# A sliding-window attention and token mixer in one kernel: the value products ordered by half with the next scores behind them, and no 64-row matrix work in token mixing

## The chip, the cores and the metric

The kernel runs on one core of a Trainium2 chip. Its time is the device time of one execution in microseconds. Five engines matter: TensorE (PE in the profile; its weight loads are listed as PEld), VectorE (DVE), ScalarE (ACT), GpSimd (POOL), and SyncE (SP), which issues most DMAs. Each engine works through its own list of instructions in the order in which the program writes them, and waits for the others by semaphores. Matrix products go to PSUM, which has eight banks here shared out to tiles by tag; a tile with one buffer must be read out before the next one of that tag is written.

## The reference

`B, H, S, D = 8, 8, 576, 64`. Attention looks back 64 positions, and its result, laid out as `x` with 8 x 576 rows of 512 channels, goes through a token mixer and a channel mixer:

```python
scores = q @ k.transpose(0, 1, 3, 2) / sqrt(D)
mask = (rel >= 0) & (rel < 64)                  # rel = row - column
attn = softmax(where(mask, scores, -1e9))
x = (attn @ v).transpose(0, 2, 1, 3).reshape(B, S, H * D)
h = relu(x.transpose(0, 2, 1) @ w_tok1) @ w_tok2        # d_tok = 256
u = x + h.transpose(0, 2, 1)
out = u + relu(u @ w_ch1) @ w_ch2                       # d_ch = 1536
```

The weights come as 64-bit floats and are converted to 32-bit ones in the kernel.

## The kernel before

The first stage (some 295 us) does attention and token mixing; the second (L574 to L621) the channel mixer, in nine chunks of 512 rows, L582 and L618 on TensorE.

The first stage goes over 36 tiles. A tile has 128 rows: two blocks of 64 positions, of one batch or, for every ninth tile (`i % 9 == 4`), the last block of each of two batches. So a pair of batches has nine tiles, and the fifth belongs half to either.

The order is written out by hand in the loop at L451 to L523, and nothing reorders it. Turn `i` of that loop mixes the work of neighbouring tiles. Before the change TensorE's list in one turn is:

- the scores of tile `i+1` (`qk`, L257, written to the two tiles `s`; 64-row, 64-column products);
- the transposition of the first half of tile `i`'s exponentials (`pt_transpose`, L292, into `pp`; ScalarE copies it to `pt`, L294); a half is four heads, even or odd ones;
- a piece of the second token product (`tok2`): transpositions of `x` (L383) and six products (L390) into the one-buffer tile `up`, which ScalarE copies to `u` (L395);
- the transposition of the second half;
- the first token product of tile `i-1` (`tok1`, L348), which needs `x` of that tile split in a high part (ScalarE, L91) and a low part (POOL, L94);
- the value products of tile `i` (`av`, L304, into `xp`), 16 of them, each on 64 columns of the array;
- a second piece.

There are 64 pieces, eight per batch. A piece of the first half covers 256 positions: two full transpositions. One of the second half covers 320: two full ones and one of 64 rows of the shared fifth tile. Where a batch ends or begins, the shared tile also enters `tok1`: one of its `tok1` products, with the low part of the weights, works on 64 rows only.

Between these, VectorE does mask and maxima (L274, L277), sums, the division by them (L318) and, in two turns of three, steps of the weight conversion (L179 to L194); ScalarE does exponentials (L285), copies and casts; POOL does low parts and a conversion step (L196). All matrix work uses 32-bit operands, with high and low parts for the token and channel products.

What the steps of the prediction touch: `av` and its heads (L302), `tok1_part` (L336 to L349), `tok2` (L378 to L384), and the place of `qk` in the loop (L466).

Of the kernel before, what the change touches and what calls it, by code (L numbers as in the profile page):

```python
# [74 lines left out]
def mixer_kernel(ctx: ExitStack, tc: tile.TileContext, qh, kh, vh, wt1, wt2, wc1, wc2, out):  # L75
# [37 lines left out]
    with ExitStack() as actx:  # L113
# [26 lines left out]
        maskr = [pa.tile([P, P], F32R, name=f"maskr{m}") for m in range(2)]  # L140
        identr = pa.tile([P, P], F32R, name="identr")
        make_identity(nc, ident)
        nc.scalar.copy(identr, ident)
        for m in (1, 0):
# [9 lines left out]
            nc.scalar.activation(maskr[m], mask[m], AF.Copy, scale=NEG_PE / NEG)  # L154

        t1hi = pa.tile([P, 5 * DT], F32R, name="t1hi")
        t1lo = pa.tile([P, 5 * DT], F32R, name="t1lo")
# [70 lines left out]
        def job_finish():  # L228
            if to_finish:
                n, w = to_finish.pop(0)  # L230
                finished.add(n)
                src, hi, lo, o, m = jobs[n]
                if hi is None:
                    nc.sync.dma_start(w2_dram[:, o:o + m], w)
                else:
                    eng = nc.vector if src is wt2 or n >= N_FIRST else nc.gpsimd
                    split(nc.scalar, eng, hi[:, o:o + m], lo[:, o:o + m], w)

        s_ps, e_sb, st = {}, {}, {}
# [59 lines left out]
        def av(i, pts):  # L299
            vt = loaded.pop(i)[1]  # L300
            xp = ps.tile([P, H, D], F32, name=f"xp{i}", tag="av", bufs=1)
            for h in range(H):  # L302
                for half in range(2):
                    nc.tensor.matmul(xp[half * BLK:(half + 1) * BLK, h],  # L304
                                     pts[h % 2][:, h // 2, half * BLK:(half + 1) * BLK],
                                     vt[:, half, h], start=True, stop=True)
            return xp
# [29 lines left out]
        def tok1_part(i, b, rows, slot, first, last):  # L337
# [3 lines left out]
            for tt in range(NTT):  # L341
                if rows is full:
                    combos = ((t1hi, xhi, full), (t1hi, xlo, full), (t1lo, xhi, full))
                else:
                    x = xhi if rows is top else xlo
                    combos = ((t1hi, x, full), (t1lo, x, rows))
                for n, (w, x, r) in enumerate(combos):
                    nc.tensor.matmul(h_ps[b][tt], w[r, slot * DT + tt * P:slot * DT + (tt + 1) * P], x[r],  # L348
                                     start=first and n == 0, stop=last and n == len(combos) - 1)  # L349
# [20 lines left out]
        def tok2(b, half, ct, hh):  # L370
# [6 lines left out]
            cs = slice(ct * P, (ct + 1) * P)  # L377
            segs = [(base + 2 * half + j, slice(0, P), j * P, P) for j in range(2)]  # L378
            if half == 1:
                r = slice(BLK, P) if odd else slice(0, BLK)  # L380
                segs.append((p * TPP + 4, r, 256, BLK))
            for j, (i, rows, o, m) in enumerate(segs):
                nc.tensor.matmul(up[:, o:o + m], xs[i][rows, cs], ident[rows, rows],  # L383
                                 start=(j == 0), stop=False, is_transpose=True, skip_group_check=True)  # L384
# [62 lines left out]
        for i in range(TOK1_FROM, NT + 1):  # L447
            m = min(n + (1 if i < TOK1_SLOW else 2), i)
            tok1_plan[i] = range(n, m)
            n = m  # L450
        for i in range(-1, NT + 1):  # L451
            if 0 <= i and i + 2 < NT:
# [12 lines left out]
            early = i < N_EARLY  # L465
            if i + 1 < NT:  # L466
                qk(i + 1)
            if 0 <= i < NT:
# [35 lines left out]
            if 0 <= i < NT:  # L504
# [3 lines left out]
                else:  # L508
                    norm(i, xp, ri)
            run_pieces(min(have, n_pieces[1]))  # L510
            for n in tok1_plan.get(i + 1, ()):
# [148 lines left out]
```

## Time and profile before

| what | value |
|---|---|
| median of 3 runs | 886.76 us (886.35 to 886.89) |
| profiled execution | 888.41 us |
| its span, first to last instruction | 886.5 us |
| mean granted TensorE clock | 0.994 |
| TensorE busy | 864.6 us, 98% of the span |
| VectorE, ScalarE, POOL busy | 372.3, 311.8, 101.4 us |

A row of the page's groups and of the answers drawn from it names the source line, engine, operation, tiles written and read, and shape; then busy time and mean length, then idle time ahead of it and who ended that. A row of the timeline gives the start in microseconds from the beginning of the span, the length, engine, line, operation, tiles, shape and count; idle time ahead of it stands in brackets with what released it. Matrix products overlap in the pipeline, so the distance from one start to the next says what a product costs, not its length. Row lengths of the chain of waits are what that step added to the chain.

### The profile page before, as it was taken

To read this page: it belongs to the slowest core of one execution; us is meant where nothing else is said; L and a number is where in the kernel's file an instruction comes from. 1 tells how busy PE (TensorE), PEld (TensorE's weight loads), DVE (VectorE), ACT (ScalarE), POOL (GpSimd) and SP (SyncE) were. 2 spreads that over 40 slices of the span, in tenths; PEclk is the share of its full clock that TensorE was granted. 3 is DMA by queue.
4 is the path that set the end of the run, shared out by engine and by line. 5 is a ranking of instruction groups with operands and counts; after the bars stand their busy time and mean duration, and the time that the engine had idled before them with its cause. 6 is when DMAs were issued, how large, how long until landed. Compare 5 with 4: busy or idle time off the path is not lost.

```text
span 886.5 us, 14562 instructions
## 1 busy us (share of the span) xinstructions
PE 864.6 (98%) x6002; PEld 708.6 (80%) x6002; DVE 372.3 (42%) x701; ACT 311.8 (35%) x966; POOL 101.4 (11%) x104
## 2 busy tenths in 40 slices
PE   7899999999999999999999999999999999999998
PEld 4667878778768888888888888888888888888887
DVE  4978777787776598130220220230220220220211
ACT  4878778778776452120120120120120220220200
POOL 2433343333332000000000000000000000000000
PEclk9989999999999999999999999999999999999999
DMA  9557566566554442100100100100100100100001
GB/s 324 188 180 248 180 229 229 196 204 225 199 175 132 130 156 90 59 1 36 60 0 36 60 1 36 60 1 36 60 12 24 60 13 24 60 13 36 0 13 36
DMA packets 39906, 84.69 MB, mean 96 GB/s; under 512 B 5280, under 2 KB 18336, under 8 KB 37920
## 3 DMA queue, kind: packets, MB, share of 16 engines
q1 hardware_dynamic: 37728, 81.93, 27.5%
q10 hardware_dynamic: 2112, 1.84, 0.6%
q8 instruction: 47, 0.77, 0.4%
q14 instruction: 19, 0.16, 0.1%
HBM read 64.09 MB, written 19.66 MB: 94 GB/s over the span
## 4 chain that ended last, share of the span: by engine, by line
PE 84%; DVE 9%; ACT 4%; issue 1%; DMA 1%; SPq 0%; POOL 0%; DVEq 0%; ACTq 0%
PE op L618 33%; PE gp L582 31%; PE up L390 5%; PE xp L304 4%; PE s L257 4%; PE h L348 3%; PE up L383 2%; ACT e L285 2%; PE pp L292 2%; DVE nm L277 1%; DVE e L274 1%; ACT pt L294 1%; DMA k<-kh 1%; DVE r L194 1%; DVE c L191 1%
## 5 line engine op out<-in xcount | busy, mean ns | idle before, releaser
L586 ACT ACTIVATE ghi<-gp 128x512 fp32r<-128x512 f32 x108 | 64.6, 598 | 440.3 <-PE gp L582 439.9
L618 PE MATMUL op<-ghi,w2lo 128*128 128x512 f32 (+1 forms) x444 | 170.3, 384 | 0.2 <-DVE w2lo L94 0.2
L618 PE MATMUL op<-ghi,w2hi 128*128 128x512 f32 (+1 forms) x444 | 170.2, 383 | 0.0
L618 PE MATMUL op<-glo,w2hi 128*128 128x512 f32 (+1 forms) x444 | 170.2, 383 | 0.0
L582 PE MATMUL gp<-uhi,w1hi 128*128 128x512 f32 x432 | 168.1, 389 | 0.0
L582 PE MATMUL gp<-ulo,w1hi 128*128 128x512 f32 x432 | 168.1, 389 | 0.0
L582 PE MATMUL gp<-uhi,w1lo 128*128 128x512 f32 x432 | 168.1, 389 | 0.0
L587 DVE SCALAR_TENSOR_TENSOR glo<-gp,ghi 128x512 fp32r<-128x512 f32 x108 | 74.6, 691 | 190.6 <-ACT ghi L586 190.6
L620 DVE TENSOR_TENSOR uf<-op,uf 128x512 f32<-128x512 f32 (+1 forms) x37 | 25.0, 677 | 242.1 <-PE op L618 242.1
L618 PEld LDWEIGHTS op<-ghi,w2lo 128*128 128x128 f32 x444 | 83.5, 188 | 17.0 <-DVE w2lo L94 0.6
L618 PEld LDWEIGHTS op<-glo,w2hi 128*128 128x128 f32 x444 | 83.5, 188 | 16.4
L618 PEld LDWEIGHTS op<-ghi,w2hi 128*128 128x128 f32 x444 | 83.5, 188 | 16.3
L285 ACT ACTIVATE e<-e,nm 128x128 f32<-128x128 f32 x232 | 90.4, 393 | 13.9 <-DVE nm L277 11.4
L582 PEld LDWEIGHTS gp<-uhi,w1lo 128*128 128x128 f32 x432 | 81.1, 188 | 16.9
L582 PEld LDWEIGHTS gp<-ulo,w1hi 128*128 128x128 f32 x432 | 81.1, 188 | 16.8
L582 PEld LDWEIGHTS gp<-uhi,w1hi 128*128 128x128 f32 x432 | 81.1, 188 | 16.8
L304 PEld LDWEIGHTS xp<-v,pt 128*64 128x64 f32 x1152 | 41.0, 143 | 21.6 <-ACT pt L294 9.5
L304 PE MATMUL xp<-v,pt 128*64 128x64 f32 x1152 | 48.7, 234 | 6.4 <-ACT pt L294 6.0
L274 DVE SCALAR_TENSOR_TENSOR e<-s,mask 128x512 f32<-128x512 f32 x58 | 39.5, 680 | 26.7 <-PE s L257 26.7
L294 ACT COPY pt<-pp 128x512 f32<-128x512 f32 x72 | 41.7, 584 | 22.1 <-PE pp L292 21.7
L94 POOL TENSOR_TENSOR xlo<-x,xhi 128x512 fp32r<-128x512 f32 x32 | 41.2, 1287 | 55.5 <-ACT xhi L91 55.3
L257 PE MATMUL s<-k,q 64*64 64x128 f32 x1152 | 45.8, 295 | 1.4 <-DMA k<-kh 0.7
(72 smaller groups left out, 1000.0 us busy)
## 6 DMA issues: line engine op xcount, KB each, us to landing
v<-vh SPq DMA_DIRECT2D x36, 512.0 KB, 3.7
raw<-wc SPq DMA_DIRECT2D x32, 384.0 KB, 4.4
q<-qh SPq DMA_DIRECT2D x36, 256.0 KB, 4.1
k<-kh SPq DMA_DIRECT2D x7, 1280.0 KB, 7.8
out<-uf SPq DMA_DIRECT2D x35, 256.0 KB, 2.3
uf<-u_dram SPq DMA_DIRECT2D x8, 1024.0 KB, 5.8
u_dram<-u SPq DMA_DIRECT2D x7, 512.0 KB, 4.5
k<-kh SPq DMA_DIRECT2D x5, 256.0 KB, 7.0
```

What stands on the lines that cost most here:

```text
L94: eng_lo.tensor_sub(lo, src, hi.bitcast(F32))
L257: nc.tensor.matmul(s[u][half * BLK:(half + 1) * BLK, j], qt[r, j, half], kbs[b][r, j, n * BLK:n * BLK + P], start=not on_pe, stop=True, sk ...
L274: nc.vector.scalar_tensor_tensor(out=e, in0=s_ps.pop((i, u)), scalar=scale, in1=mk.unsqueeze(1).to_broadcast([P, 4, P]), op0=ALU.mult, op1 ...
L285: nc.scalar.activation(e[:, h], src[:, h], AF.Exp, bias=nm[:, g:g + 1], scale=by, accum_out=sm[:, g:g + 1])
L294: nc.scalar.copy(pt, pp)
L304: nc.tensor.matmul(xp[half * BLK:(half + 1) * BLK, h], pts[h % 2][:, h // 2, half * BLK:(half + 1) * BLK], vt[:, half, h], start=True, sto ...
L348: nc.tensor.matmul(h_ps[b][tt], w[r, slot * DT + tt * P:slot * DT + (tt + 1) * P], x[r], start=first and n == 0, stop=last and n == len(co ...
L390: nc.tensor.matmul(up[:, :n], hx[:, cs], w[:, tt * S + s0:tt * S + s0 + n], start=False, stop=(k == 6), skip_group_check=True)
L582: nc.tensor.matmul(gp, w[:, ct * F + ft * P:ct * F + (ft + 1) * P], x[:, ct], start=(k == 0), stop=(k == 3 * NCT - 1))
L586: nc.scalar.activation(ghi, gp, AF.Relu)
L587: nc.vector.scalar_tensor_tensor(out=glo, in0=gp, scalar=0.0, in1=ghi.bitcast(F32), op0=ALU.max, op1=ALU.subtract)
L618: nc.tensor.matmul(op, w[:, ct, ft], x[:, cols], start=(k == 0), stop=(k == 3 * NFT - 1))
```

## The change

Two things are changed at once.

The value products of a tile are issued with all even heads first, then all odd ones. Even heads need the first transposed half, odd heads the second. And the scores of tile `i+2` are issued at the end of turn `i`, between its value products and its second piece, where the scores of tile `i+1` stood at the start of turn `i+1`, behind that piece. (The scores of tile 0 go ahead of the loop.)

TensorE around the value products of tile 10, before (`xp` value products, `up` a piece, `s12` scores of tile 12, `pp11` a transposition of exponentials; the third and fourth value rows go on in turn):

```order
L304 MATMUL xp10_1338<-v10_1016,pt10_0_1281 64x64 x2
L304 MATMUL xp10_1338<-v10_1016,pt10_1_1315 64x64 x2
...
L383 MATMUL up0_1_3_1357<-ident_65,x2_528 128x128
L383 MATMUL up0_1_3_1357<-ident_65,x3_583 128x128
L383 MATMUL up0_1_3_1357<-ident_65,x4_689 128x64
L390 MATMUL up0_1_3_1357<-t2hi_129,hhi0_0_764 128x320
...
L257 MATMUL s12_0_1380<-k2_703,q12_1136 64x128 x2
L257 MATMUL s12_1_1381<-k2_703,q12_1136 64x128 x2
...
L292 MATMUL pp11_0_1398<-ident_65,e11_0_1285 128x128 x4
L383 MATMUL up1_0_0_1419<-ident_65,x5_799 128x128
```

The same place after:

```order
L313 MATMUL xp10_1345<-v10_1041,pt10_0_1288 64x64 x8
L313 MATMUL xp10_1345<-v10_1041,pt10_1_1322 64x64 x8
L266 MATMUL s12_0_1364<-k2_730,q12_1161 64x128 x2
L266 MATMUL s12_1_1365<-k2_730,q12_1161 64x128 x2
...
L393 MATMUL up0_1_3_1382<-ident_65,x2_533 128x128
L393 MATMUL up0_1_3_1382<-ident_65,x3_590 128x128
L393 MATMUL up0_1_3_1382<-ident_65,x4_696 128x128
L400 MATMUL up0_1_3_1382<-t2hi_134,hhi0_0_771 128x320
...
L301 MATMUL pp11_0_1405<-ident_65,e11_0_1292 128x128 x4
L393 MATMUL up1_0_0_1426<-ident_65,x5_806 128x128
```

The scores stand ahead of the piece now; between it and the next piece (`up1_0_0`) only `pp11_0` is left, and the third transposition has 128 columns.

Token mixing has no 64-row work any more. The third transposition of a second-half piece takes all 128 rows of the shared tile, against the identity or, for the odd batch, a matrix with its halves exchanged (`swapped`); the 64 columns that belong to the other batch are written and not used. In `tok1`, the low part of the weights for the shared tile stands in `t1z`, zero in the other 64 rows, so that this product takes all 128 rows too. TensorE at the shared tile 13, before:

```order
L348 MATMUL h2_0_1320<-xhi13_1715,t1hi_127 128x512
L348 MATMUL h2_0_1320<-xhi13_1715,t1lo_128 128x512
L348 MATMUL h2_1_1321<-xhi13_1715,t1hi_127 128x512
L348 MATMUL h2_1_1321<-xhi13_1715,t1lo_128 128x512
L348 MATMUL h3_0_1917<-xlo13_1716,t1hi_127 128x512
L348 MATMUL h3_0_1917<-xlo13_1716,t1lo_128 128x512
```

and the rows for the second of the two batches after:

```order
L358 MATMUL h3_0_1924<-xlo13_1741,t1hi_132 128x512
L358 MATMUL h3_0_1924<-xlo13_1741,t1z_130 128x512
L358 MATMUL h3_1_1925<-xlo13_1741,t1hi_132 128x512
L358 MATMUL h3_1_1925<-xlo13_1741,t1z_130 128x512
L358 MATMUL h3_0_1924<-xhi14_1870,t1hi_132 128x512
```

Count and place of the products are the same; those of `t1lo` read 64 rows before, those of `t1z` read 128. POOL makes the new constants: two copies and a memset in the setup, and two casts behind the last low part of the token weights:

```order
L94 TENSOR_TENSOR t1lo_133<-w2_364,t1hi_132 128x320
L94 TENSOR_TENSOR xlo1_439<-x1_431,xhi1_438 128x512
L202 TENSOR_TENSOR w3_466<-r3_465,c3_449 128x320
L94 TENSOR_TENSOR t1lo_133<-w3_466,t1hi_132 128x320
L246 CAST t1z_130<-t1lo_133 64x256 x2
L94 TENSOR_TENSOR xlo2_543<-x2_533,xhi2_542 128x512
```

They stand ahead of the low part of tile 2. The lists of ScalarE and VectorE keep their order.

```diff
+        swapped = pa.tile([P, P], F32, name="swapped")
...
+        for c in range(2):
+            nc.gpsimd.tensor_copy(swapped[:, c * BLK:(c + 1) * BLK], ident[:, (1 - c) * BLK:(2 - c) * BLK])
+
+        t1z = pa.tile([P, 2, DT], F32R, name="t1z")
+        nc.gpsimd.memset(t1z.bitcast(F32), 0.0)
...
+                    if src is wt1 and o + m == 5 * DT:
+                        for c, r in enumerate((top, bottom)):
+                            nc.gpsimd.tensor_copy(t1z[r, c], t1lo[r, 4 * DT:].bitcast(F32))
...
-            for h in range(H):
+            for h in [*range(0, H, 2), *range(1, H, 2)]:
...
-                    combos = ((t1hi, xhi, full), (t1hi, xlo, full), (t1lo, xhi, full))
+                    combos = ((t1hi, xhi), (t1hi, xlo), (t1lo, xhi))
                 else:
                     x = xhi if rows is top else xlo
-                    combos = ((t1hi, x, full), (t1lo, x, rows))
-                for n, (w, x, r) in enumerate(combos):
-                    nc.tensor.matmul(h_ps[b][tt], w[r, slot * DT + tt * P:slot * DT + (tt + 1) * P], x[r],
+                    combos = ((t1hi, x), (None, x))
+                for n, (w, x) in enumerate(combos):
+                    w, o = (t1z[:, rows is bottom], 0) if w is None else (w, slot * DT)
+                    nc.tensor.matmul(h_ps[b][tt], w[:, o + tt * P:o + (tt + 1) * P], x,
...
-            segs = [(base + 2 * half + j, slice(0, P), j * P, P) for j in range(2)]
+            segs = [(base + 2 * half + j, ident, j * P) for j in range(2)]
             if half == 1:
-                r = slice(BLK, P) if odd else slice(0, BLK)
-                segs.append((p * TPP + 4, r, 256, BLK))
-            for j, (i, rows, o, m) in enumerate(segs):
-                nc.tensor.matmul(up[:, o:o + m], xs[i][rows, cs], ident[rows, rows],
+
+                segs.append((p * TPP + 4, swapped if odd else ident, 256))
+            for j, (i, perm, o) in enumerate(segs):
+                nc.tensor.matmul(up[:, o:o + P], xs[i][:, cs], perm,
...
+        qk(0)
         for i in range(-1, NT + 1):
...
-            if i + 1 < NT:
-                qk(i + 1)
...
+            if i + 2 < NT:
+                qk(i + 2)
             run_pieces(min(have, n_pieces[1]))
```

## The prediction

> **What bounds the kernel now.** The page came first: busy shares, then the chain that ended last.
>
> ```profile
> PE 864.6 (98%) x6002; PEld 708.6 (80%) x6002; DVE 372.3 (42%) x701; ACT 311.8 (35%) x966; POOL 101.4 (11%) x104
> PE 84%; DVE 9%; ACT 4%; issue 1%; DMA 1%; SPq 0%; POOL 0%; DVEq 0%; ACTq 0%
> ```
>
> TensorE is busy for 98% of the span, but the lines that the change touches (scores L257, value products L304, token products L348, transpositions L383) run only in the first third. So the second view is the busy time by stretch: two single periods (from one tile's scores to the next tile's), then two long stretches.
>
> ```profile
> 69.57:76.73 7.16, 6.76 (x95) 5.71 (x94) 6.05 (x13) 5.38 (x21) 3.23 (x3) 1.00 0.52 167
> 84.52:92.27 7.75, 7.75 (x97) 6.31 (x96) 5.88 (x13) 5.63 (x21) 2.23 (x2) 1.00 0.53 183
> 62.43:183.04 120.61, 117.92 (x1527) 96.55 (x1523) 92.97 (x185) 94.88 (x352) 43.25 (x38) 1.00 0.63 210
> 183.04:294.60 111.56, 107.66 (x1266) 87.42 (x1266) 79.53 (x153) 81.27 (x284) 35.84 (x32) 0.98 0.58 194
> ```
>
> Columns are length, then PE, PEld, DVE, ACT, POOL busy, granted clock, DMA. From 62 to 295 us TensorE is nearly always busy, VectorE and ScalarE for three quarters. There are two kinds of period: light (7.16 us, two pieces of the first half) and heavy (7.75 us, two pieces of the second half, which hold the 64-row transposition). Being busy is not the same as advancing, so the third view is the timeline, where start-to-start distances count. The heavy period:
>
> ```profile
> 84.28 0.31 PE L390 MATMUL up<-t2hi,hlo 128*128 128x320 f32 x1
> 84.52 1.10 PE L257 MATMUL s<-k,q 64*64 64x128 f32 x32
> 85.56 0.66 PE L292 MATMUL pp<-ident,e 128*128 128x128 f32 x4
> 86.05 0.59 PE L383 MATMUL up<-ident,x 128*128 128x128 f32 x3
> 86.82 0.31 PE L390 MATMUL up<-t2lo,hhi 128*128 128x320 f32 x1
> 86.36 0.14 PEld L383 LDWEIGHTS up<-ident,x 64*128 64x128 f32 x1 [0.17 <-issue]
> 89.46 1.24 PE L304 MATMUL xp<-v,pt 128*64 128x64 f32 x32
> 90.63 0.64 PE L383 MATMUL up<-ident,x 128*128 128x128 f32 x3
> 92.03 0.31 PE L390 MATMUL up<-t2hi,hlo 128*128 128x320 f32 x1
> ```
>
> The light period:
>
> ```profile
> 71.10 0.38 PE L383 MATMUL up<-ident,x 128*128 128x128 f32 x2
> 71.44 0.28 PE L390 MATMUL up<-t2lo,hhi 128*128 128x256 f32 x1
> 72.03 0.60 PE L292 MATMUL pp<-ident,e 128*128 128x128 f32 x4
> 72.39 0.48 PE L348 MATMUL h<-xhi,t1hi 128*128 128x512 f32 x1
> 72.70 0.39 PE L348 MATMUL h<-xlo,t1hi 128*128 128x512 f32 x1
> 72.93 0.40 PE L348 MATMUL h<-xhi,t1lo 128*128 128x512 f32 x1
> 73.96 0.34 PE L304 MATMUL xp<-v,pt 128*64 128x64 f32 x4
> 74.69 1.03 PE L304 MATMUL xp<-v,pt 128*64 128x64 f32 x28 [0.40 <-ACT pt L294]
> 75.66 0.44 PE L383 MATMUL up<-ident,x 128*128 128x128 f32 x2
> 76.52 0.28 PE L390 MATMUL up<-t2hi,hlo 128*128 128x256 f32 x1
> ```
>
> **The transposition without 64 rows.** With three transpositions, the last on 64 rows, the first transposition and the second product lie 0.77 us apart (86.05 to 86.82). With two full ones it is 0.34 (71.10 to 71.44). A third full one adds about 0.11 (four L292 rows end to end, less the last one's length: (0.60-0.27)/3) and the wider first product 0.02: 0.47. So each of the 32 pieces concerned gains 0.30 us: 24 in twelve heavy periods, 8 after the last scores. The 64-row weight load waits 0.17 us for nothing the trace names; the rest stands between it and the next product.
>
> The Trainium skill, TensorE: Matmul & The Clock Gate, section "Why this matters for your kernels", speaks against this: products of few rows that land in different row groups run at the same time, so narrow work would be the cheap kind. Here nothing ran beside the 64-row rows (0.77 against 0.34). By the page this term would be a small loss, not 0.30 a piece.
>
> **The token products of half tiles.** Four rows alternate 128 and 64 rows, here after a wait for POOL:
>
> ```profile
> 254.14 0.50 PE L348 MATMUL h<-xhi,t1hi 128*128 128x512 f32 x1 [0.39 <-POOL xhi L330]
> 254.57 0.50 PE L348 MATMUL h<-xhi,t1lo 64*128 64x512 f32 x1
> ```
>
> They follow each other at 0.43 us, full rows at 0.23 (72.70 to 72.93). A group of four gains 0.80, eight groups (two per pair of batches) 6.4. But the wait ahead shows that POOL, ScalarE or the next value products set the end in some of them. Bounds 1.6 to 6.4; I take half, 3.2.
>
> **The next scores behind the value products.** The change takes the scores from behind the second piece to ahead of it. Undisturbed value products with scores right behind:
>
> ```profile
> 61.35 1.15 PE L304 MATMUL xp<-v,pt 128*64 128x64 f32 x32
> 62.43 1.10 PE L257 MATMUL s<-k,q 64*64 64x128 f32 x32
> ```
>
> That is 1.08 us, with no more gap than value products then transpositions have. One change of shape goes away: product to scores takes 0.24 (84.28 to 84.52) against a product's pace of 0.145, and the four L292 rows behind scores 0.66 against 0.60. Gain 0.15 a period. Nothing is issued but matrix rows; no DMA is moved, nor any row of POOL's, SP's, ScalarE's or VectorE's queues. The inputs of the scores are loaded more than a period ahead.
>
> The cost is a new wait. The bank of the pieces ("up") exists once. Today scores and L292 stand between the second piece and the next first one; now L292 alone. ScalarE's rows, the copy in this heavy period and the one before it with a weight cast:
>
> ```profile
> 84.63 0.43 ACT L395 COPY u<-up 128x320 f32<-128x320 f32 x1 [0.26 <-PE up L390]
> 84.95 0.62 ACT L91 CAST xhi<-x 128x512 fp32r<-128x512 f32 x1
> 78.52 0.59 ACT L294 COPY pt<-pp 128x512 f32<-128x512 f32 x1 [0.26 <-PE pp L292]
> 79.00 0.52 ACT L91 CAST w1hi<-w 128x384 fp32r<-128x384 f32 x1
> 79.41 0.40 ACT L285 ACTIVATE e<-e,nm 128x128 f32<-128x128 f32 x1
> 80.97 0.41 ACT L395 COPY u<-up 128x320 f32<-128x320 f32 x1
> 81.28 0.58 ACT L294 COPY pt<-pp 128x512 f32<-128x512 f32 x1
> 78.33 1.28 POOL L94 TENSOR_TENSOR xlo<-x,xhi 128x512 fp32r<-128x512 f32 x1 [0.25 <-ACT xhi L91]
> ```
>
> The copy ends 0.78 us after the last product starts (84.28 to 85.06); L292 is through after 0.15+0.43. So the next first piece waits 0.22 (0.17 with the narrower copy), and L292's second half, token and value products queue behind it.
>
> **Value products by half.** Today they stop after four rows for the second copy: 1.70 us from 73.96 to the transposition at 75.66, against 1.08 undisturbed: 0.62 a light period; in the heavy one 1.17 (89.46 to 90.63), a loss of 0.09. Now the first half (0.47) runs during that copy. Whether the stall goes depends on the copy. Scores earlier by a piece let VectorE (6.05 us busy of 7.16) start its maxima earlier. Then ScalarE's own line-up decides: second piece's copy, cast of x, copy of pt, weight cast, exponentials, first piece's copy, second copy of pt. From the second piece's last product that is 0.35 (84.28 to 84.63) + 0.32 (to 84.95) + 0.52 (0.62 less the overlap seen between neighbours) + 0.48 + 0.41 + 1.56 + 0.31 + 0.58 + 0.05 = 4.58; then the second half of the value products 0.47, change of shape 0.15, scores 1.04 (84.52 to 85.56), and the second piece 1.10 (90.63 to 92.03 less 0.30). This ring is 7.34 us. For a light period it is 4.45+0.47+0.15+1.04+0.86 = 6.97.
>
> Without the weight cast (about two periods in five) other things end last. Heavy: TensorE's own work, 7.75-0.60-0.15-0.09+0.22 = 7.13. Light: the low half of x. It is ready 0.33+0.27+0.62+0.08+1.28 = 2.58 after the last product, and TensorE wants it after 0.12+0.44+0.17+0.93+0.36+0.31 = 2.33, so it stalls 0.25: 7.16-0.62-0.15+0.17+0.25 = 6.81. Today x is ready earlier because the copy ahead of its cast is; that is the stall that comes next.
>
> Sum over the periods: heavy 8x0.41 + 4x0.62 = 5.8; light 5x0.19 + 5x0.35 = 2.7 (two longer light ones are in the token term).
>
> **Setup.** Two copies and a memset on POOL stand ahead of its first addition, for which it waits long anyway; without that cover, three rows no longer than the one below (0.87) would add up to 2.6 us. Two casts into t1z (64x256) stand ahead of a low half of x on POOL, in the stretch where VectorE sets the end:
>
> ```profile
> L94 POOL TENSOR_TENSOR t1lo<-w,t1hi 128x320 fp32r<-128x320 f32 x4 | 3.5, 867 | 8.2 <-ACT t1hi L91 8.2
> 36.19 1.16 DVE nm L272
> 28.24 0.35 DVE nm L272
> ```
>
> By t1lo each cast is at most 0.69 (867 ns x 256/320). The small VectorE row L272 took 1.16 beside POOL's work there, 0.35 elsewhere. So the casts cost between -0.8 (the small row slips in between) and 1.4; I take 0.4.
>
> **The sum.** 5.8 + 2.7 + 3.2 + 2.4 (8x0.30, pieces after the last scores, where the chain is TensorE alone) - 0.4 = 13.7 us. The profiled execution took 888.41, its span 886.5, so it would come to 874.7; the median of the runs shown is 886.76, and the same off it gives **873.1**. The channel stage behind (L582, L618) starts earlier and keeps its length.
>
> **Rivals.** *TensorE's sum comes true entire*: no ring, no waits. 12x0.84 + 10x0.77 + 6.4 + 2.4 + 0.8 = 27: 860. Against it: a 7.34 ring needs only rows that exist. 12%.
>
> *The rings are longer than reckoned*, light periods gain nothing, heavy ones 0.2, token groups a quarter: 2.4+1.6+2.4-1.2 = 5: 881.5. For it: VectorE is busy 6.05 of 7.16 us and may deliver late. 18%.
>
> *Slower: the low half of x.* Its POOL row now falls on VectorE's weight conversion. If the two hold each other up as L272 shows (0.8 us), and the token products wait 1.2 us for it in each of some 16 periods with a conversion, 19 us go: 892. From 1.0 us a period it decides. Against it: VectorE also starts earlier. 6%.
>
> *Narrow work costs nothing of itself*, the page's rule as a mechanism here: the 0.30 stays when the rows are full, so the 64-row terms vanish, wider rows add 32x0.05, and of the order only the light 2.7 is left, heavy periods going even: about 886, no change. The page is the TensorE page of the Trainium skill named above. The 0.77 against 0.34 speaks against it. 3%.
>
> **Chances and range.** My forecast has 61%, from 868 to 878 by itself. The half clock granted for some microseconds where TensorE had waited (0.98 in the last long stretch) may come at other places, 1 or 2 us either way. The range takes the larger part of the two neighbours: 864 to 881.5. A run tells 0.2%, or 1.8 us, from no change: faster 0.89, same 0.04, slower 0.07.
>
> **What would show it.** First transposition to second product 0.47 in heavy pieces; half-tile token rows at 0.23; value products with no stop after four rows; a wait of about 0.2 at L393 for the copy of u; periods near 7.1 to 7.35 and 6.8 to 7.0. Wrong if light periods stay at 7.16 with a new stall at the low half of x, or if the copy of u comes late behind exponentials.

## The result, and the profile after

The changed kernel takes 879.46 us (median; 878.17 to 881.3) where the kernel before took 886.83 us in runs beside it. The ratio is 0.9918, with a 95% interval of 0.9903 to 0.9933: 7.4 us faster. The forecast was 873.1 us, 13.7 us faster, so the sign was right, the time lies in the range (864 to 881.5) near its upper end, and nearly half of the expected gain is missing. The profiled execution took 880.53 us, its span 878.7.

The page's busy shares and the chain that ended last, of the changed kernel:

```profile
PE 850.6 (97%) x6002; PEld 702.6 (80%) x6002; DVE 378.3 (43%) x701; ACT 307.5 (35%) x966; POOL 105.3 (12%) x109
PE 83%; DVE 8%; ACT 4%; POOL 2%; issue 2%; DMA 1%; POOLq 0%; SPq 0%; DVEq 0%; ACTq 0%
```

TensorE has 14.0 us less work (864.6 before), about what was predicted as the gain, but the span fell by 7.8 only: the rest went into waiting. POOL has entered the chain with 2%.

Busy time by stretch, before, then after. The first row of each runs from the end of the value products of tile 24 to that of tile 31 (seven periods whose token products take no shared tile); the second from the first product of chunk 0 of the channel stage to that of chunk 1. The third row of after lies inside its second. Columns as in the prediction.

```profile
197.88:249.84 51.96, 50.82 (x673) 42.08 (x669) 38.82 (x80) 40.70 (x152) 17.22 (x15) 1.00 0.59 204
294.46:360.23 65.77, 65.59 (x290) 53.99 (x289) 50.26 (x106) 22.48 (x44) 0.00 (x0) 1.00 0.32 104
```

```profile
191.21:241.71 50.50, 49.73 (x672) 41.19 (x669) 42.96 (x81) 40.37 (x158) 18.35 (x16) 1.00 0.64 210
283.36:352.44 69.08, 67.22 (x291) 55.15 (x289) 50.05 (x106) 21.94 (x44) 0.00 (x0) 0.98 0.38 116
324.00:328.00 4.00, 4.00 (x11) 3.17 (x12) 3.83 (x10) 0.58 (x2) 0.00 (x0) 0.57 0.24 84
```

The first stage ends 11.10 us earlier (283.36 against 294.46), but the first chunk behind it takes 3.31 us longer. The other chunks keep their length to 0.01 us.

Where a period's time goes is seen in the timeline. This is a light period (both its pieces are of the first half) of the changed kernel, from the last product of its second piece on (tile 25):

```profile
193.27 0.28 PE L400 MATMUL up<-t2hi,hlo 128*128 128x256 f32 x1
193.59 0.37 ACT L405 COPY u<-up 128x256 f32<-128x256 f32 x1 [1.34 <-PE up L400]
193.86 0.62 ACT L91 CAST xhi<-x 128x512 fp32r<-128x512 f32 x1
194.56 1.43 POOL L94 TENSOR_TENSOR xlo<-x,xhi 128x512 fp32r<-128x512 f32 x1 [4.72 <-ACT xhi L91]
195.36 0.47 PE L358 MATMUL h<-xhi,t1hi 128*128 128x512 f32 x1
196.05 0.50 PE L358 MATMUL h<-xlo,t1hi 128*128 128x512 f32 x1 [0.21 <-POOL xlo L94]
197.41 1.15 PE L313 MATMUL xp<-v,pt 128*64 128x64 f32 x32
198.49 1.10 PE L266 MATMUL s<-k,q 64*64 64x128 f32 x32
```

The value products run through, 1.08 us from start to the next scores: their stall is gone. Instead the product of the low half starts 0.69 us behind the one ahead of it, where 0.23 is the pace: a stall of 0.46. Read upwards: the low half waits for its difference on POOL, that for the cast of x on ScalarE, and the cast stands behind the copy of u, for which ScalarE had idled 1.34 us. The product on TensorE that the copy wants comes a scores block later than it used to. The waits for POOL's xlo, by the weight loads, have grown from 2 to 19 (before, then after; columns: us in total, times, longest):

```profile
PEld h L348 <- POOL xlo L94: 2.2, 2, 1.2
```

```profile
PEld h L358 <- POOL xlo L94: 9.6, 19, 1.2
```

For a budget, the table gives the start of each group of TensorE rows to the start of the next group, summed over those seven periods (tiles 24 to 31); a wait ahead of a group counts with the group before it. The granted clock was full in all of these stretches. All kernels of the study that bear on it are in it; e1 to e10 are explained below.

```
us in seven periods      pieces  scores  score transp.  token   value   sum
before                    18.02    7.25      5.94       10.97    9.79   51.96
after                     15.80    7.25      7.02       12.76    7.68   50.50
e2  64-row work only      16.01    7.24      5.93       10.98   10.94   51.10
e5  by half only          18.02    7.25      5.93       10.95    8.32   50.47
e6  scores moved only     17.83    7.24      7.01       12.36    8.25   52.70
e1  both orders           17.83    7.25      7.01       12.26    7.57   51.92
e7  both orders + split   17.83    7.25      7.01       11.00    7.60   50.69
e3  after + split         15.84    7.25      7.33       10.99    7.60   49.00
e9  after - scores moved  15.99    7.24      5.93       11.04    8.48   48.68
e10 e9 + split            16.23    7.25      6.97       10.97    8.28   49.71
```

After against before: pieces -2.2, value products -2.1, but score transpositions +1.1 (the piece behind them waits for the copy of u) and token products +1.8 (the late low half).

The start of the channel stage, changed kernel, by the timeline:

```profile
284.02 0.52 ACTq L420 DMA_DIRECT2D u_dram<-u  x1
286.37 0.60 ACT L597 ACTIVATE ghi<-gp 128x512 fp32r<-128x512 f32 x1 [2.38 <-PE gp L593]
291.24 0.55 ACT L175 ACTIVATE c<-raw 128x384 f32<-128x384 f32 x1 [4.28 <-DMA u_dram<-u]
291.69 0.58 ACT L597 ACTIVATE ghi<-gp 128x512 fp32r<-128x512 f32 x1
323.94 0.50 PE L629 MATMUL op<-ghi,w2lo 128*128 128x512 f32 x1 [1.86 <-DVE w2lo L94]
```

In the kernel before, the same rows stood without that wait:

```profile
295.12 0.52 ACTq L410 DMA_DIRECT2D u_dram<-u  x1
297.40 0.60 ACT L586 ACTIVATE ghi<-gp 128x512 fp32r<-128x512 f32 x1 [2.31 <-PE gp L582]
297.89 0.54 ACT L169 ACTIVATE c<-raw 128x384 f32<-128x384 f32 x1
```

ScalarE's row c does not read u. Its output shares memory with the tile of u that is being stored. The two new tiles (2.5 KB per partition) shift the first stage's tiles, and the compiled program has one more wait there, for the queue of that store: DMAHW6 alone before, now

```
L175 ACTIVATE c27_4425<-raw27_4402 128x384 [waits DMAHW6_49,DMAHW5_49]
```

ScalarE stands at it for 4.28 us, VectorE's weight conversion waits 4.1 us for it, and 33 us later TensorE waits 1.86 us for w2lo. Half clock follows (0.57 in the stretch from 324 to 328 above). The Trainium skill, TensorE: Matmul & The Clock Gate, "What's actually happening", lets the clock fall after an idle window of about 3.4 us; here one wait of 1.86 us stood ahead of it, and in e2_rows below 2.1 us at the same place brought none.

### The profile page after: what moved, and what is told of

It is laid out like the page before. It is cut to its first block, busy times and chain, and to the rows that moved or that the text cites. A ratio compares the mean times of both kernels' runs of the same rounds, so it can differ in the third digit from the quotient of the medians.

```text
span 878.7 us, 14566 instructions
## 1 busy us (share of the span) xinstructions
PE 850.6 (97%) x6002; PEld 702.6 (80%) x6002; DVE 378.3 (43%) x701; ACT 307.5 (35%) x966; POOL 105.3 (12%) x109
## 4 chain that ended last, share of the span: by engine, by line
PE 83%; DVE 8%; ACT 4%; POOL 2%; issue 2%; DMA 1%; POOLq 0%; SPq 0%; DVEq 0%; ACTq 0%
PE op L629 33%; PE gp L593 30%; PE h L358 5%; PE up L400 4%; PE s L266 4%; PE xp L313 3%; PE up L393 2%; POOL xlo L94 2%; PE pp L301 1%; ACT u L405 1%; DVE r L200 1%; DMA u_dram<-u 1%; DVE c L197 1%; ACT xhi L91 1%; ACT e L294 1%
## 5 line engine op out<-in xcount | busy, mean ns | idle before, releaser
L313 PEld LDWEIGHTS xp<-v,pt 128*64 128x64 f32 x1152 | 37.4, 137 | 16.4 <-ACT pt L303 6.3
L266 PE MATMUL s<-k,q 64*64 64x128 f32 x1152 | 43.7, 287 | 2.4 <-DVE c L197 1.9
L313 PE MATMUL xp<-v,pt 128*64 128x64 f32 x1152 | 43.1, 226 | 2.7 <-ACT pt L303 2.4
L294 ACT ACTIVATION_READ_ACCUMULATOR e<-e,nm 128x1 f32 x232 | 44.8, 193 | 0.0
```

The source lines that it names most:

```text
L266: nc.tensor.matmul(s[u][half * BLK:(half + 1) * BLK, j], qt[r, j, half], kbs[b][r, j, n * BLK:n * BLK + P], start=not on_pe, stop=True, sk ...
L294: nc.scalar.activation(e[:, h], src[:, h], AF.Exp, bias=nm[:, g:g + 1], scale=by, accum_out=sm[:, g:g + 1])
L313: nc.tensor.matmul(xp[half * BLK:(half + 1) * BLK, h], pts[h % 2][:, h // 2, half * BLK:(half + 1) * BLK], vt[:, half, h], start=True, sto ...
```

## The experiments

Theory: the orders work on TensorE as predicted, but the cast of x stands behind the second piece's copy on ScalarE, and moving the scores ahead of that piece makes both late; beside that, the new tiles' place costs the first chunk 3.3 us. First rival: VectorE and POOL hold each other up, so x is late wherever its cast stands. Second rival: the channel stage's start is bound by VectorE's weight conversion and loses whatever an earlier start gains.

**The two orders alone (e1_order).**

```
-            for h in range(H):
+            for h in [*range(0, H, 2), *range(1, H, 2)]:
...
+        qk(0)
         for i in range(-1, NT + 1):
...
-            if i + 1 < NT:
-                qk(i + 1)
...
+            if i + 2 < NT:
+                qk(i + 2)
             run_pieces(min(have, n_pieces[1]))
```

> The kernel before with the two changes of order alone: the value products by half and the scores block behind them. The 64-row work stays, and so does the layout of the memory. My theory is that both orders take the wait of the value products away (0.62 us in a light period), that the low half of x is late afterwards because its cast stands behind the copy of the second piece on ScalarE (0.2 to 0.5 us of stall on the token products of a period), and that the first chunk of the channel stage, whose 3.3 us loss in the changed kernel comes from the two new tiles' place in memory, is not touched here: 882 to 884.5 us, with the wait of c27 on ScalarE below 0.5 us and the token products that stall on xlo as in the changed kernel. The first rival (VectorE and POOL hold each other up, whatever the order) gives the same stall in the changed kernel and in the kernel before, so no gain: 886 to 887. The second rival (the channel stage's start loses what any earlier start gains, since VectorE's conversion of the weights bounds it) gives a first chunk longer by whatever the first stage is shorter: 886 to 887 too, but with the end of the first stage 3 us earlier.

Measured: 888.16 us, ratio 1.0016 (1.0006 to 1.0027): the orders alone gain nothing; the time is 3.7 us above the upper end of the expectation. The budget shows why: the value products take 2.2 us less, and the token products and the wait for the copy of u take 2.4 more. Outside the seven periods, those of tiles 32 and 33 take 2.2 us more than before, behind a wait of 1.57 us for POOL's half tile and with half clock from 252.6 to 259.5 us. The first rival has the same stall with either order; here it is the order that moves it. The second rival has no support either: the first chunk keeps its 65.77 us. ScalarE's copies and casts in the seven periods, before and e1_order (the number behind the bar: busy us, mean ns; then the idle time just ahead):

```profile
L395 ACT COPY u<-up 128x256 f32<-128x256 f32 (+1 forms) x14 | 5.4, 388 | 2.9 <-PE up L390 2.9
L91 ACT CAST xhi<-x 128x512 fp32r<-128x512 f32 x7 | 4.4, 622 | 0.2 <-DVE x L318 0.2
```

```profile
L395 ACT COPY u<-up 128x256 f32<-128x256 f32 (+1 forms) x14 | 5.5, 392 | 11.6 <-PE up L390 11.6
L91 ACT CAST xhi<-x 128x512 fp32r<-128x512 f32 x7 | 4.4, 622 | 0.0
```

Nearly all of ScalarE's idle time (11.6 of 12.2 us) now stands ahead of the copy of u. The Trainium skill, TensorE: Matmul & The Clock Gate, "Architectural detail: the array is 16× 32×32, not 1× 128×128", calls ScalarE's queue strict first in, first out; these rows agree: the cast waits for nothing of its own (0.0) while the copy ahead of it waits 11.6 us.

**The 64-row work alone (e2_rows)** is the changed kernel with the two orders undone, as in the diff above read backwards.

> The kernel before with the 64-row work alone replaced; both orders as before. By my theory the PE work shrinks by 0.30 us in each of 32 pieces of token mixing (9.6 us), of which the 8 pieces behind the last tile show in full (2.4 us) and those under a period that PE bounds show in part, and the half-tile token products give up to 3.2 us; the first chunk of the channel stage loses about 3 us through the place of the two new tiles, with the wait of c27 on ScalarE above 3 us: 881.5 to 884.5 us in all. If the loss at the channel stage came from the orders and not from the tiles, the wait would be missing here and the time 879 to 881.5.

Measured: 883.68 us, ratio 0.9961 (0.9946 to 0.9976), inside the expectation. The pieces give 2.0 us in the seven periods, but the value products' stall takes 1.15 of it back: they reach ScalarE's second copy of pt earlier and wait longer. That is why this part and the value products by half are worth more together than apart. The first chunk took 1.94 us longer, with

```profile
ACT c L175 <- DMA u_dram<-u: 4.5, 1, 4.5
PE op L628 <- DVE w2lo L94: 2.1, 1, 2.1
```

The granted clock stayed at 1.00 through this chunk, though TensorE waited longer here than in the changed kernel.

**The casts of x ahead of the second piece (e3_split)**, in the changed kernel:

```
+            for n in tok1_plan.get(i + 1, ()):
+                if n not in xhl:
+                    split_x(n)
             run_pieces(min(have, n_pieces[1]))
-            for n in tok1_plan.get(i + 1, ()):
-                if n not in xhl:
-                    split_x(n)
```

> The changed kernel with the casts and differences of x (split_x) written ahead of the second piece of token mixing, so that the cast stands ahead of that piece's copy on ScalarE. My theory (the low half is late because of the cast's place) says that the stall of the token products on xlo goes below 0.1 us in the periods without a shared tile, and that the time falls by 2 to 5 us from 879.5 to 874.5 to 877.5; the piece's copy then comes up to 0.9 us later and may hold up the next piece, which is why not all of the stall is gained. The first rival (VectorE and POOL hold each other up, so that x itself comes late) says that the cast waits for x wherever it stands: the stall stays at 0.2 to 0.5 us and the time within 1 us of the changed kernel's 879.5.

Measured: 873.92 us, ratio 0.9855 (0.9838 to 0.9872), 5.5 us below the changed kernel and 0.6 below the expected band. The token products are back at 10.99 us, ScalarE's idle time ahead of the copy of u is 3.5 us where it was 8.2, and the low half waits 4 times instead of 19. The first rival falls. Not all of the 5.5 us is the cast's: the first chunk is shorter too, 66.83 us for 69.08, with a wait of 3.6 us at c27, one of 1.2 at w2lo, and no half clock. What the cast alone is worth is read from e8_place_split against e4_place, where neither has that wait: 4.0 us. ScalarE's rows in the seven periods, e3_split and then the changed kernel:

```profile
L405 ACT COPY u<-up 128x256 f32<-128x256 f32 (+1 forms) x14 | 5.5, 390 | 3.5 <-PE up L400 3.5
L91 ACT CAST xhi<-x 128x512 fp32r<-128x512 f32 x7 | 4.3, 620 | 2.0 <-DVE x L327 2.0
```

```profile
L405 ACT COPY u<-up 128x256 f32<-128x256 f32 (+1 forms) x14 | 5.5, 392 | 8.2 <-PE up L400 8.2
L91 ACT CAST xhi<-x 128x512 fp32r<-128x512 f32 x7 | 4.4, 622 | 0.0
```

**Another place for c27 (e4_place)**, in the changed kernel, ahead of w2lo:

```
+        abs_of[N_FIRST] = pb.tile([P, CW], I32, name=f"c{N_FIRST}", tag="cvc", bufs=2)[:, :jobs[N_FIRST][4]]
         w2lo = pb.tile([P, NCT, NFT, P], F32R, name="w2lo")
...
-                abs_of[n] = pb.tile([P, CW], I32, name=f"c{n}", tag="cvc", bufs=2)[:, :m]
+                if n not in abs_of:
+                    abs_of[n] = pb.tile([P, CW], I32, name=f"c{n}", tag="cvc", bufs=2)[:, :m]
```

> The changed kernel with the first converted row of the channel stage (c27) and its second buffer allocated ahead of w2lo, so that they no longer lie over the last tile of u that is being stored; nothing else differs, and the store's tile then lies under VectorE's glo0_1, as in the kernel before. My theory says that ScalarE's wait at c27 falls from 4.3 us to below 0.5, that PE's 1.9 us wait for w2lo goes and the half clock behind it with it, and that the time falls by 2 to 3.3 us to 876 to 877.5. The second rival (VectorE's conversion of the weights bounds that start, and it waits for the same stores anyway) says that the wait moves to VectorE and that the time stays within 0.7 us of 879.5.

Measured: 876.59 us, ratio 0.9886 (0.9869 to 0.9903), 2.9 us below the changed kernel. The wait of c27 is gone, TensorE waits 0.2 us for w2lo, and the first chunk has its old length at full clock, with a start as early as 284.27:

```profile
284.27:350.05 65.78, 65.60 (x290) 53.99 (x289) 50.25 (x106) 22.49 (x44) 0.00 (x0) 1.00 0.34 105
PE op L631 <- DVE w2lo L94: 0.2, 1, 0.2
```

The second rival falls with it.

**The value products by half alone (e5_half)**: only the first pair of lines of e1_order's diff.

> The kernel before with the value products by half alone; the scores block stays at the head of its period and the 64-row work stays. My theory, as it stands after the first four runs, is that the scores block behind the value products is what makes the cast of x late (it puts 1.03 us of PE work between the value products and the second piece, and the copy of that piece stands ahead of the cast on ScalarE), and that the value products by half only take their own stall away: the token products then stay near 11.0 us in the seven periods from tile 24 to tile 31, the value products fall from 9.8 to about 7.6, and the time is 880 to 884 us. The rival, suggested by the orders alone that gave nothing (51.92 us for those seven periods against 51.96): the round trip through ScalarE has a fixed length that neither order touches, so that what the value products lose in stalls comes back elsewhere; those seven periods then stay within 0.4 us of 51.96 and the time is 886 to 888.

Measured: 880.58 us, ratio 0.994 (0.9926 to 0.9954). The token products stay at 10.95 us; the value products come down to 8.32, not to 7.6: about 0.25 us of stall is left in a light period.

**The scores moved alone (e6_scores)**: the rest of that diff.

> The kernel before with the scores block moved behind the value products, and nothing else. My theory says that the move alone makes the low half of x late and leaves the stall of the value products where it is or in part: the token products of tiles 24 to 31 grow from 10.97 to over 12 us, the periods grow or stay, 52 to 53 us for the seven, and the time is 887 to 890. The rival of the fixed round trip gives 51.9 for the seven periods and 886 to 887.5.

Measured: 891.59 us, ratio 1.0049 (1.0036 to 1.0063), 1.6 us worse than the upper end. The token products take 12.36 us. So the move by itself costs 5 us, and the two orders nearly cancel in e1_order: alone, one gains 6.0 and the other loses 5.0.

**Both orders with the casts ahead (e7_order_split).**

> The two orders of e1_order with the casts and differences of x written ahead of the second piece, as in e3_split; the 64-row work stays. My theory (the orders gave nothing in e1_order because the cast of x stands behind the copy of the second piece) says that the token products of tiles 24 to 31 go back from 12.3 to 11.0 us and the seven periods fall from 51.9 to 50.5 or below, the time to 881 to 884 us. The rival of the fixed round trip leaves the seven periods at 51.5 to 52 and the time at 885.5 to 888; it would also say that the split was worth 5.5 us behind the changed kernel only because the 64-row work was gone.

Measured: 880.51 us, ratio 0.9933 (0.9919 to 0.9948): 7.7 us below e1_order, 0.5 below the expected band, and no 64-row work was touched. The token products are back at 11.0 us. The rival of a fixed round trip is out; the cast's place is what moving the scores spoils.

**Both repairs (e8_place_split)**: e4_place with e3_split's diff.

> The changed kernel with both repairs: c27 allocated elsewhere (e4_place) and the casts of x ahead of the second piece (e3_split). The first-stage end of e3_split (15.1 us ahead of the kernel before, at the first product of the channel stage) is kept, and its loss of 1.06 us in the first chunk goes: 871.5 to 873.5 us. If the two repairs hit the same time (an earlier end of the first stage meets VectorE's weight conversion), 873.5 to 876.

Measured: 872.57 us (872.11 to 873.06), ratio 0.9842 (0.983 to 0.9855). The first stage ends as early as in e3_split (278.27 us, there 279.37) and the first chunk is back at 65.78 us, so an early end of the first stage meets no bound there. Together the repairs give 6.9 us where apart they gave 5.5 and 2.9, since the first chunk of e3_split was already 2.25 us shorter than the changed kernel's. By its median this is the fastest kernel of the study, 14.0 us below the kernel before; the interval of e9_noscores_place overlaps with its own.

**The scores back at the head of the period (e9_noscores_place)**: e4_place with the lines on qk as before.

> e4_place with the scores block put back to the head of its period; the value products by half, the work without 64 rows and the place of c27 stay. My theory, as the first eight runs leave it, is that the scores block behind the value products only costs: it adds the wait of a token mixing piece for the copy of u (0.15 us per period, 1.07 in the seven periods from tile 24 to tile 31) and the late low half of x (1.8 us in them). Without it I expect the score transpositions and pieces' waits of those seven periods back at 5.9 us and the token products at 11.0, the value products at 8.3 to 9.5 (they had 7.6 with the scores moved), the seven periods at 48.3 to 49.5 us, and the time at 868 to 873 us. The rival says that with the 64-row work gone ScalarE's round trip is the bound and the scores' place only says where PE waits: the value products then take 10.5 to 11, the seven periods stay at 50.3 to 50.7 and the time at 875.5 to 877.5.

Measured: 873.81 us, ratio 0.9857 (0.9839 to 0.9876). The seven periods, 48.68 us, are in the expected band and the shortest of all; the time is 0.8 above its band. The profile shows the period of tile 33 1.5 us longer than in the kernel before; the clock was granted at 0.70 from 248 to 252 us, behind stalls of the token products:

```profile
248.00:252.00 4.00, 3.15 (x22) 1.97 (x23) 2.57 (x5) 3.73 (x18) 1.09 (x1) 0.70 0.14 49
```

Against e4_place (876.59) only the scores' place differs: the moved scores cost 2.8 us inside the changed kernel. Against e8_place_split (872.57), where the scores are moved and the casts stand ahead of the piece, no difference is clear. So the move costs while the casts stand behind the piece, and with the casts ahead it is not shown to gain or lose.

**The same with the casts ahead (e10_noscores_place_split).**

> e9_noscores_place with the casts and differences of x ahead of the second piece of token mixing, as in e8_place_split. By my theory the casts are in time already without the moved scores (two waits for xlo and 2.2 us in the kernel before), so the split repairs nothing here: within 1.5 us of e9_noscores_place, to either side, since the copy of the second piece comes 0.6 to 0.9 us later and what reads it has time. If the casts' place matters whatever the order (the rival to what e7_order_split showed), it gains 3 us or more.

Measured: 879.45 us, ratio 0.9912 (0.9895 to 0.9929): 5.6 us slower than e9, which neither expectation had. The same edit that gained 4.0 us behind the moved scores (e8 against e4) loses here. With the scores at the head, the copy of u is due early and the cast is the one that waits: ScalarE stands 2.0 us at the casts for VectorE's x, and the copy of u behind them comes late for the next piece. First e9, then e10, in the seven periods:

```profile
L406 ACT COPY u<-up 128x256 f32<-128x256 f32 (+1 forms) x14 | 5.4, 383 | 0.9 <-PE up L401 0.9
L91 ACT CAST xhi<-x 128x512 fp32r<-128x512 f32 x7 | 4.4, 622 | 0.5 <-DVE x L328 0.3
```

```profile
L406 ACT COPY u<-up 128x256 f32<-128x256 f32 (+1 forms) x14 | 5.4, 386 | 0.0
L91 ACT CAST xhi<-x 128x512 fp32r<-128x512 f32 x7 | 4.3, 619 | 2.0 <-DVE x L328 2.0
```

TensorE's piece waits show it: the score transpositions with the wait behind them are 6.97 us, 1.04 more than in e9. In the profiled executions 2.25 us more lie in the period of tile 6, where e10 was granted half clock from 51.8 to 58.7 us and e9 full clock behind waits of the same length (1.93 and 1.94 us), so the order's share is less than the whole difference.

**The place alone (e11_unused)**: the kernel before with

```
+        unused = pa.tile([P, 640], F32, name="unused")
+        nc.gpsimd.memset(unused, 0.0)
         t1hi = pa.tile([P, 5 * DT], F32R, name="t1hi")
```

> The kernel before with one unused tile of 2.5 KB per partition, cleared once on POOL, where the changed kernel has its two new tiles; all else as before. By my theory this alone moves c27 onto the last tile of u that is being stored: the first chunk of the channel stage is 1 to 3.3 us longer (from the first product of chunk 0 to the first of chunk 1, 65.77 us in the kernel before), with ScalarE's wait at c27 over 2 us, 887.5 to 890 us. If the loss there came from the earlier end of the first stage and not from the place, it stays at 65.8 and the time within 0.7 us of the kernel before.

Measured: 886.7 us, ratio 0.9997 (0.9987 to 1.0007): no change, a miss. The wait is there, but the chunk is only 0.45 us longer (66.22 us):

```profile
ACT c L171 <- DMA u_dram<-u: 3.0, 1, 3.0
PE op L620 <- DVE w2lo L94: 0.6, 1, 0.6
292.49:358.71 66.22, 65.61 (x291) 53.98 (x289) 50.08 (x106) 22.47 (x44) 0.00 (x0) 1.00 0.39 122
```

The four kernels with the wait line up: 3.0 us at c27 gives 0.6 at w2lo, 3.6 (e3_split) gives 1.2, 4.3 (after) 1.9, 4.5 (e2_rows) 2.1. The conversion has 2.4 us of slack, and only what is longer is paid. So the place costs 0.45 us in the kernel before, 1.06 in e3_split, 1.94 in e2_rows and 3.31 in the changed kernel; only there did half clock follow the stall, though e2_rows stalled longer. Why the wait's length varies from 3.0 to 4.5 us was not settled.

## Why the prediction was right or wrong

By the profiled spans the 7.8 us are made up as follows, each from the ends of the value products (first stage) or the first products (channel stage): to tile 5 -3.2; the 22 periods of the heavy/light term -4.8; the seven periods with a half tile -1.1; the pieces after the last scores -2.0; the first chunk +3.3.

**Transposition and tail: right.** 0.30 us a piece was predicted; in e9 against before the heavy period of tile 10 has its pieces at 1.36 and 1.20 us for 1.65 and 1.50, so 0.29 and 0.30. The tail gave 2.0 of 2.4. The rival that narrow work costs nothing of itself, with no change of the time, is refuted by e2_rows.

**The step that failed most is "Without the weight cast ... other things end last".** For periods with a weight cast the length given by the ring through ScalarE came true: 6.97 us predicted for light ones, 6.97 measured at tiles 8 and 12 (7.06 and 7.08 at 20 and 29); 7.34 for heavy ones, 7.34 and 7.35 at tiles 18 and 27. In part this may be luck: in the light ones the value products run through at 1.08 us, and what TensorE is seen to wait for is again the low half of x (0.3 us at tile 8). For light periods without a cast the prediction had 6.81, and 7.14 and 7.13 was measured at tiles 16 and 25 (7.12 and 7.13 before): nothing gained. Tile 25 before and after, in the prediction's terms: value products -0.59 (predicted -0.62), wait for the copy of u +0.14 (0.17), change of shape -0.03 (-0.15), low half of x +0.48 (0.25). The stall was seen and named, but at half its size, and the saved change of shape was not there: the piece ahead of the scores fell by 0.09 and the other one rose by 0.06. Of the stall, POOL's row is a part (1.43 us, not 1.28). Heavy periods without a cast, "TensorE's own work, 7.13", took 7.30 (tile 10) and 7.52 (tiles 22 and 31); there too the token products stalled, 0.27 us at the last two, and this was not in the prediction. In all 8.5 us were predicted for these periods and 4.8 came. The prediction's count was off as well: it has twelve heavy and ten light periods, but of the 22 only five hold two pieces of the second half and six two of the first, nine hold one of each, and two (tiles 7 and 34) a single piece. The nine mixed ones gained 0 to 0.41 us each, 1.7 in all.

The prediction counted the moved scores as a gain (0.15 a period) with one wait (0.22). The wait came at its size; the gain did not, and a second wait sat behind it in ScalarE's queue. "Nor any row of ScalarE's queue is moved" was true and misled: the row kept its place, but what its head waits for came 1.03 us later.

**Half tiles: the rows right, the hiding not.** The rows of half tiles follow at 0.23 us as predicted, and TensorE saves 0.60 and 0.80 per pair of batches (1.72 to 1.12 for four rows, 3.28 to 2.48 for ten at tile 15), 5.6 over four pairs. Of 6.4 the prediction kept half, 3.2; 1.1 came. One of the seven periods, that of tile 6, took 1.1 us longer than before (10.64 us), with a wait of 1.92 us ahead of the scores that the kernel before does not have; both kernels had half clock there (51.3 to 58.2 us, before 51.5 to 58.4). With the same wait and full clock e1_order took 8.59 us and e9 8.48, so what of this is the change's is open. The other six gave 2.2. In two of these the shared tile's cast stands behind the same copy, here at tile 22:

```profile
178.50 0.62 ACT L338 CAST xhi<-x 64x512 fp32r<-64x512 f32 x1
179.26 1.43 POOL L339 TENSOR_TENSOR xhi<-x,xhi 64x512 fp32r<-64x512 f32 x1 [3.29 <-ACT xhi L338]
180.74 0.50 PE L358 MATMUL h<-xhi,t1hi 128*128 128x512 f32 x1 [1.72 <-POOL xhi L339]
```

That wait is 1.72 us here (1.73 at tile 31); it was 0.38 and 0.39 at these tiles before, and there is none in e3_split.

**"The channel stage behind starts earlier and keeps its length": wrong, 3.3 us.** The lines of the change say nothing of it; the memory that two pools use in turn does. With the place repaired (e4_place) the statement holds to 0.01 us.

**Setup: the casts near what was reckoned, the start open.** A cost of 0.4 us was reckoned. In the seven kernels with the new constants the period of tile 4, at whose start the two casts hold up POOL's low half of tile 2, takes 8.95 to 8.98 us, in the six others 8.69 to 8.71: 0.27 us. The first five tiles came out 3.2 us earlier all the same. About 1.0 of it is the period of tile 5 (6.82 us for 7.83), and that goes with the orders: 6.81 to 6.84 in the kernels with the value products by half (7.38 in e5_half), 7.83 to 7.92 in the four without. Most of the rest is the start: the value products of tile 0 end at 18.3 us in the profile of before, the latest of all thirteen, and at 15.9 in that of the changed kernel, the earliest; in e11_unused, whose program up to there differs from the kernel before by one clear on POOL, at 17.2. So up to 2.4 of the 7.8 us between these two profiles can be a start that differs from one execution to the next, and not the change. What the start-up is worth is open.

**Rivals.** "The rings are longer than reckoned" (881.5) comes nearest in time, but not by its mechanism: VectorE did not deliver late. "Slower: the low half of x" had the right place and, in the main, the wrong cause. Rows of VectorE and POOL that ran beside each other were longer here: beside the POOL row of 1.43 us at tile 25, a conversion row of VectorE took

```profile
194.88 1.32 DVE L188 TENSOR_SCALAR c<-c 128x384 int32<-128x384 int32 x1
```

where the five rows of this line (L182 there) took 0.36 us each in the mean of the seven periods before. But x itself was on time (ScalarE's casts wait 0.0 us for it), and e3_split, where such rows of VectorE are long too (42.3 us busy in the seven periods, 43.0 in the changed kernel, 38.8 before), has no stall left. The cast came late, and it cost up to 0.5 us a period, not 1.0.

## What to carry to other kernels

Moving one engine's work moves every row of another engine's queue that waits for it, and all that is queued behind: for each moved block, look up the first row that now waits longer on each other engine, and what stands behind that row. Which of two rows should stand first in such a queue depends on which of their inputs is ready first, so an order that is right for one placement (e8_place_split against e4_place, -4.0 us) is wrong for the other (e10 against e9, +5.6 us, a part of it half clock). And when a change adds tiles, list the waits of the next stage's first rows in the program of both kernels: memory taken over from a tile that is still being stored shows up there, and nowhere in the diff.

## What the runs showed of the hardware that was not expected

Half clock came around waits of TensorE that were shorter than the half clock itself, and not each time. In the changed kernel some 3.4 us at half clock (0.57 in the mean from 324 to 328 us) followed a wait of 1.86 us; 3.31 - 1.86 leaves 1.45 us for the slower clock. In e2_rows a wait of 2.11 us at the same product was followed by full clock. In the period of tile 6 the changed kernel, e3_split, e4_place and e10 had half clock for 6.9 us around a wait of 1.92 to 1.94 us, e1_order and e9 none around the same wait; the kernel before had it there too, where its longest wait was 1.16 us. What decides is not shown, so a stall of this length belongs in a forecast's range both with and without half clock behind it. The two runs of the changed kernel with a mean granted clock of 0.993 took 880.5 and 881.3 us, those with 0.996 and 0.998 took 878.2 and 878.4, so the spread of a kernel's own runs goes with such windows.

POOL's row for the low half of x took 1.28 us (mean over seven) in the kernel before and in e3_split, where its cast is in time, and 1.37 in the changed one, up to 1.52; the VectorE row beside one of 1.43 us took 1.32 us for 0.36. Which of the two holds up the other was not tried.
